# A long convolution and a soft mixture of experts on one core: x buffers no longer cleared, tables and clearings later, and the loads of a pair of steps in two bursts

## The chip, the cores and the metric

The kernel runs on one core of a Trainium2 chip. The metric is the device time of one execution in microseconds (us); lower is better. Before the change, three runs took 909.87, 915.80 and 915.04 us; their median is 915.04 us.

## The reference

A causal convolution along the sequence with a filter as long as the sequence, and then a soft mixture of experts with 8 experts of 4 slots each, all in float32:

```python
# x (8, 5696, 128), h (5696, 128)
Xf = np.fft.rfft(x, n=2 * S, axis=1); Hf = np.fft.rfft(h, n=2 * S, axis=0)
y = np.fft.irfft(Xf * Hf[None], n=2 * S, axis=1)[:, :S, :].reshape(B * S, D)
logits = y @ phi                                   # (45568, 32)
d = softmax of logits over the tokens              # columns
slot_input = d.T @ y                               # (32, 128), then per expert
slot_out[e] = np.maximum(slot_input[e] @ w1[e], 0) @ w2[e]
out = (softmax of logits over the slots) @ slot_out
```

## The kernel before, in words

The transform of length 5760 is done as 90 x 64 (`N1` x `N2`): stage A transforms over the 89 rows (`R1`) that hold data, stage B over the 64 columns, multiplies with the filter's spectrum and transforms back over the 64, and stage C transforms back over the 90 and goes on to the logits. There are nine groups: group 0 is the filter `h`, groups 1 to 8 are the eight sequences.

**Steps.** The main loop (L631) runs over steps `t`. In step `t` stage A takes one chunk of four columns, eight steps (`NJ`) to a group, 72 in all. Stage B runs nine steps behind (`LAG_B`): a group has twelve units (`NW`), one in an odd step and two in an even step. Stage C runs 27 steps behind and takes one pair of steps for one block of output, and four pairs make a sequence. The last blocks and the experts come after the loop. So an odd and an even step are one pair, with three units of stage B, two chunks of stage A and one block of stage C.

**Where data lies between stages.** `load_x` brings the input of a pair into one of two buffers `xc`, and GpSimd folds each chunk into one of three buffers `x` (`fold`, L217: the sum and the difference of a near and a far half). `stage_a` multiplies (L241), ScalarE copies the results out of PSUM (L243), and `pending` collects their stores to the array `f` in HBM, which `flush` issues: two of 60 rows in each step ("f60") and four more of 30 rows in odd steps ("f30"). `load_g` loads one unit of `f` into one of three buffers `gt` (L270). `stage_b1` multiplies it (L284) and VectorE applies the filter; `stage_b2` multiplies back (L327), and its result is stored to `zm` or, for the last units of a group, in four small stores to `zr`. `load_main` and `load_rest` bring these into `zc` and `zx` for stage C (L412, L417).

**What sets the order.** The code is issued in the order that is written, and each engine runs its own instructions in that order. Nearly every DMA is issued from SyncE's queue (SP), in the order of the code, and one that has to wait holds up all that are behind it. In the built program the DMAs use eight semaphores in turn, so that a DMA also waits for the landing of the one that used its semaphore before. `prefetch` (L638) issues a `gt` load three units ahead: unit u+3 goes into the buffer of unit u, and so stands behind `stage_b1(u)`. A group's `gt` loads may begin at the last step of the group before in stage B, for only then is all of the group's `f` on its way.

**SP's order in a pair, before.** Even step: `load_rest` of some pairs, the load of `xc`, f60 x2, `gt`, `zm` x2, the store of stage C's weights (L562), `gt`, `zm` x2. Odd step: f60 x2, `zc`, `zx`, `gt`, `zm` x2, f30 x4.

**The beginning.** Both `xc` buffers are cleared on VectorE (L176), since `h` fills only 89 of 128 rows. SP then loads `h` and the tables `wt` (L618, for `stage_b1`) and `vt` (L619, for `stage_b2`). ScalarE's queue loads `s1` and small tables, and copies a cleared tile into the rows of `zr` that are never written (L625, eight DMAs).

Of the kernel before, what the change touches and what calls it, by code (L numbers as in the profile page):

```python
# [70 lines left out]
def kernel(  # L71
# [24 lines left out]
    nc = tc.nc  # L96
    P = 128
# [5 lines left out]
    N1, N2 = 90, 64  # L103
    R1, HALF, NP = S // N2, N2 // 2, N1 // 2
    CH = 4
    NJ = HALF // CH
# [54 lines left out]
    wt = fconst.tile([P, NP, HP], F32, name="wt")  # L161
    vt = fconst.tile([P, NU, 2, HP], F32, name="vt")
# [9 lines left out]
    xs = {}  # L172
    xf = [apool.tile([P, 2, CH, D], F32, name=f"x{i}", tag=f"x{i}", bufs=1) for i in range(3)]
    xcs = [apool.tile([P, 2, 2 * CH, D], F32, name=f"xc{i}", tag=f"xc{i}", bufs=1) for i in range(2)]
    for t_ in xcs:
        nc.vector.memset(t_[:, :, :, :], 0.0)  # L176

    def load_x(m, halves=((0, 2 * CH),)):

        if 2 * m >= (B + 1) * NJ:  # L180
            return
        g, j = divmod(2 * m, NJ)
        if g == 0:
            src, blocks = h, ((0, R1 // 16 * 16), (R1 // 16 * 16, R1))
        else:
            r0 = min((g - 1) * R1, B * R1 - XR) * N2
            src, blocks = x.rearrange("b t d -> (b t) d")[r0:r0 + XR * N2], ((0, XR),)
        src = src.rearrange("(a n) d -> a n d", n=N2)
        t_ = xcs[m % len(xcs)]
        for n0, n in halves:  # L190
            a = (CH * j + n0, N2 - CH * j - n0 - n)
            p = (n0, 2 * CH - n0 - n)
            for r0, r1 in blocks:
                if n == 2 * CH:
                    v = src[r0:r1, a[0]:a[0] + n, :]
                    v = bass.AP(tensor=v.tensor, offset=v.offset,
                                ap=[v.ap[0], [(a[1] - a[0]) * D, 2], [1, n * D]])
                    nc.sync.dma_start(
                        out=t_[r0:r1, :, :, :].rearrange("p s n d -> p s (n d)"), in_=v)
                    continue  # L200
                for s_ in range(2):
                    nc.sync.dma_start(
                        out=t_[r0:r1, s_, p[s_]:p[s_] + n, :].rearrange("p n d -> p (n d)"),
                        in_=src[r0:r1, a[s_]:a[s_] + n, :].rearrange("r n d -> r (n d)"))
        xs[2 * m] = xs[2 * m + 1] = t_

# [2 lines left out]
    def fold(c):  # L209
        if c not in xs:  # L210
            return
        t_ = xs.pop(c)
        y_ = xf[c % len(xf)]
        i = CH * (c % 2)
        near, far = t_[:, 0, i:i + CH, :], t_[:, 1, ::-1, :][:, i:i + CH, :]
        for o in range(2):
            nc.gpsimd.tensor_tensor(out=y_[:, o, :, :], in0=near, in1=far,  # L217
                                    op=AL.subtract if o else AL.add)
        folded[c] = y_

# [2 lines left out]
    def flush():  # L223
        while pending:
            pending.pop(0)()
# [375 lines left out]
    NA, NC = (B + 1) * NJ, B * NJ  # L601
# [10 lines left out]
    AHEAD = 3  # L612
# [2 lines left out]
    load_x(0, ((0, CH), (CH, CH)))  # L615
    nc.scalar.dma_start(out=s1[:, :, :, :], in_=t_s1)
    load_x(1)
    nc.sync.dma_start(out=wt[:, :, :], in_=t_w)  # L618
    nc.sync.dma_start(out=vt[:, :, :, :], in_=t_v)  # L619
    nc.scalar.dma_start(out=phi[:, :], in_=moe_phi)  # L620
    nc.scalar.dma_start(out=turn[:, :, :, :, :], in_=t_turn)
    nc.scalar.dma_start(out=im[:, :, :], in_=t_im)
    nc.scalar.dma_start(out=ir[:, :], in_=t_ir)
    for i in range(8):
        nc.scalar.dma_start(  # L625
            out=zr[i // 4][i // 2 % 2, i % 2, N1 - MAIN:].rearrange("k (j r) d -> (k j) (r d)", r=2 * CH),
            in_=zring[0][1][0:4 * (HALF - N1 + MAIN), :, :, :].rearrange("p h n d -> p (h n d)"))
    fold(0)
    wait_b2 = []

    for t in range(last_front + 1):  # L631
        us = list(units(t))

        def pair(lag):
            T, half = divmod(t - LAG_C - lag, 2)
            return T if half == 0 and 0 <= T < NT else None

        def prefetch(last):  # L638
            nonlocal loaded
            while loaded < len(queue) and queue[loaded][0] <= last \  # L640
                    and queue[loaded][0] // NW * NJ + NJ <= t:
                load_g(queue[loaded][0])
                loaded += 1

        def slot_b(due=True):
            fresh = due and bool(us)
            if fresh:
                u = us.pop(0)
                stage_b1(u)
                prefetch(u + AHEAD)  # L650
                wait_b2.append(u)
            if len(wait_b2) > fresh:
                stage_b2(wait_b2.pop(0))

        T, U, V, W, X = [pair(k) for k in (0, 2, 1, 3, 5)]
        if t < NA:
            stage_a(t, False)
            fold(t + 1)
        if t == last_front:
            assert T is None and U is None  # L660
            assert pair(-1) % NQ
            flush()
            dispatch(W)
            for i in range(3):
                slot_b()
                flush()
                if i == 1:
                    softmax_sum(W)
                    stage_c2(V)
            assert not us and not wait_b2  # L670
            stage_c6(X)
            stage_c3(V)
            column_max(V)
            break
        if t % 2:
            if T is not None:
                stage_c1(T)()
            flush()
            if pair(-2) is not None:
                load_main(pair(-2))  # L680
                if pair(-2) % NQ:
                    load_rest(pair(-2))
            slot_b()
            if U is not None:
                stage_c4(U)
            if t < NA:
                stage_a(t, True)
            if U is not None:
                stage_c5(U)
                softmax_exp(U)  # L690
            flush()
        else:
            if pair(-1) is not None and pair(-1) % NQ == 0:
                load_rest(pair(-1))
            if t < NA:
                load_x(t // 2 + 2)
            flush()
            if t == NJ:
                prefetch(AHEAD - 1)
            slot_b()  # L700
            if W is not None:
                softmax_sum(W)
                dispatch(W)
            flush()
            if V is not None:
                stage_c2(V)
            if X is not None:
                stage_c6(X)
            slot_b()
            if V is not None:  # L710
                stage_c3(V)
# [221 lines left out]
```

## Time and profile before

The profiled execution took 909.23 us by the clock that gives the times above; its span in the trace is 907.4 us.

| what | value |
|---|---|
| TensorE matmuls (PE) | 760.2 us, 84% of the span |
| VectorE (DVE) | 601.4 us, 66% |
| ScalarE (ACT) | 436.8 us, 48% |
| GpSimd (POOL) | 399.8 us, 44% |
| DMA | 278.33 MB, mean 307 GB/s |
| HBM | read 147.94 MB, written 129.00 MB |

| DMA, all on SP | count | KB each |
|---|---|---|
| `gt<-f` | 99 | 512 |
| `f<-fst`, 60 rows | 144 | 240 |
| `f<-fst`, 30 rows | 144 | 120 |
| `zm<-zst` | 128 | 256 |
| `zc<-zm` | 30 | 1024 |
| `zx<-zr` | 30 | 512 |
| `xc<-in_x_dram` | 32 | 768 |
| `zr<-zst` | 96 | 128 |
| `wt<-tab_w`, `vt<-tab_v` | 1 each | 1440, 1472 |

The eight clearings `zr<-zx`, of 96 KB each, are issued from ScalarE's queue.

A group of instructions is named by engine, output and line: "PE bt L284" is the matmul of `stage_b1`. An engine's name with a q is its queue: "SPq L270" is the issue of a `gt` load. "x<-y" after DMA is a transfer from y to x. In a list of waits, the three numbers are the time waited in all, the number of waits and the longest one. In a table by windows, PE, PEld, DVE, ACT and POOL have their busy time and the number of instructions, followed by the granted clock of TensorE, the busy share of the DMA engines (packets that overlap count twice, so it can pass 1) and the rate in GB/s.

### The profile page before, as it was taken

Reading aid. Unit: us, or ns where it says so; the run is one execution under the profiler, and the core shown is the slowest. Engines: PE = TensorE matmul, PEld = TensorE weight load, DVE = VectorE, ACT = ScalarE, POOL = GpSimd, SP = SyncE. Lnnn points to the kernel's source line nnn. Section 1 sums busy time; section 2 is a strip of 40 time slices with the busy share of each in tenths; the row PEclk is TensorE's granted clock in tenths of the full one; section 3 lists DMA queues with packets and bytes.
Section 4 is the critical chain, followed back from the end, with each engine's and each line's share of the span. In section 5 each row is a group of like instructions: output and inputs, shape, how many; then the busy total and the mean of one; then the engine's idle time right before and its main releaser. Section 6 shows DMA issues by size and latency. Waiting matters only on the chain.

```text
span 907.4 us, 21291 instructions
## 1 busy us (share of the span) xinstructions
PE 760.2 (84%) x8308; PEld 387.7 (43%) x8308; DVE 601.4 (66%) x896; ACT 436.8 (48%) x880; POOL 399.8 (44%) x353
## 2 busy tenths in 40 slices
PE   6857778689999989999998999799888877767893
PEld 2212233234444444444444444344444434344793
DVE  2029767568778867886877787678778766653552
ACT  2423234335556545665655655456544444563441
POOL 4634322444555655655655566456332224651000
PEclk9979889999999999999999999899988888766855
DMA  8989999999999999999999999999998768540798
GB/s 267 318 275 343 293 296 337 298 314 376 341 291 375 361 326 308 372 358 299 357 364 335 295 373 348 303 308 346 306 291 304 264 200 341 186 166 1 292 406 335
DMA packets 170443, 278.33 MB, mean 307 GB/s; under 512 B 13543, under 2 KB 128231, under 8 KB 165135
## 3 DMA queue, kind: packets, MB, share of 16 engines
q1 hardware_dynamic: 169336, 275.74, 89.7%
q10 hardware_dynamic: 1008, 1.25, 0.5%
q8 instruction: 66, 1.08, 0.5%
q14 instruction: 33, 0.27, 0.1%
HBM read 147.94 MB, written 129.00 MB: 305 GB/s over the span
## 4 chain that ended last, share of the span: by engine, by line
PE 47%; DMA 23%; ACT 8%; POOL 8%; DVE 6%; issue 6%; SPq 1%; ACTq 0%; DVEq 0%; POOLq 0%
PE bank L241 9%; DMA gt<-f 9%; PE bt L284 9%; PE bz L327 6%; POOL y L430 5%; PE bank L412 4%; DMA f<-fst 4%; PE op L886 3%; PE bank L439 3%; PE bank L417 3%; PE bank L448 2%; DMA zx<-zr 2%; ACT fst L243 2%; DMA out_dram<-o 2%; PE bank L527 2%
## 5 line engine op out<-in xcount | busy, mean ns | idle before, releaser
L241 PE MATMUL bank<-x,s 128*32 128x512 f32 (+1 forms) x1152 | 218.0, 620 | 12.9 <-POOL x L217 8.4
L217 POOL TENSOR_TENSOR x<-xc 128x512 f32<-128x512 f32 x144 | 180.4, 1278 | 107.2 <-PE bank L241 86.5
L284 PE MATMUL bt<-gt,wt 64*64 64x256 f32 x1620 | 125.0, 419 | 72.8 <-DMA gt<-f 33.0
L430 POOL TENSOR_TENSOR y<-y,op 128x512 f32<-128x512 f32 x64 | 77.6, 1213 | 206.8 <-DVE op L404 204.3
L304 DVE TENSOR_TENSOR pi<-bt,Hi 128x1024 f32<-128x1024 f32 x96 | 113.0, 1177 | 83.5 <-PE bt L284 83.3
L243 ACT ACTIVATE fst<-bank 128x512 f32<-128x512 f32 x216 | 122.8, 592 | 86.0 <-PE bank L241 57.7
L332 ACT ACTIVATE zst<-bz 128x1024 f32<-128x1024 f32 x96 | 93.3, 972 | 128.3 <-PE bz L327 109.4
L284 PEld LDWEIGHTS bt<-gt,wt 64*64 64x64 f32 x1620 | 58.3, 141 | 151.2 <-issue 79.1
L312 DVE TENSOR_TENSOR yf<-bt,pi 128x512 f32<-128x512 f32 x192 | 119.4, 663 | 3.3
L304 DVE TENSOR_TENSOR bt<-bt,Hr 128x1024 f32<-128x1024 f32 x96 | 113.0, 1177 | 0.0
L241 PEld LDWEIGHTS bank<-x,s 128*32 128x32 f32 (+1 forms) x1152 | 55.1, 126 | 129.8 <-issue 93.6
L327 PE MATMUL bz<-yf,vt 64*64 64x256 f32 x1440 | 110.4, 404 | 0.0
L327 PEld LDWEIGHTS bz<-yf,vt 64*64 64x64 f32 x1440 | 64.3, 143 | 25.5 <-issue 4.2
L512 POOL TENSOR_TENSOR L<-L,rs 128x512 f32<-128x512 f32 x32 | 33.5, 1048 | 91.6 <-DVE rs L511 66.4
L404 DVE TENSOR_TENSOR y<-bank,y 128x512 f32<-128x512 f32 x32 | 22.1, 692 | 76.7 <-ACT y L420 76.5
L439 PE MATMUL bank<-ident,y 109*128 109x109 f32 x512 | 62.7, 273 | 7.9 <-ACT yt L441 7.9
L504 ACT ACTIVATE L<-L 128x512 f32<-128x512 f32 x32 | 20.2, 630 | 94.7 <-POOL L L501 94.6
L430 POOL TENSOR_TENSOR y<-y,om 128x512 f32<-128x512 f32 x54 | 63.9, 1183 | 2.1
L439 PEld LDWEIGHTS bank<-ident,y 109*128 109x128 f32 x512 | 52.9, 149 | 19.4 <-POOL x L217 14.7
L412 PE MATMUL bank<-zc,im 64*64 64x512 f32 x480 | 60.8, 623 | 0.0
L441 ACT ACTIVATE yt<-bank 128x360 f32<-128x360 f32 x128 | 53.0, 482 | 7.7 <-PE bank L439 7.3
L420 ACT ACTIVATE y<-bank 128x512 f32<-128x512 f32 x32 | 19.1, 596 | 72.6 <-PE bank L417 72.6
(101 smaller groups left out, 862.5 us busy)
## 6 DMA issues: line engine op xcount, KB each, us to landing
gt<-f SPq DMA_DIRECT2D x99, 512.0 KB
f<-fst SPq DMA_DIRECT2D x144, 240.0 KB
zm<-zst SPq DMA_DIRECT2D x128, 256.0 KB
zc<-zm SPq DMA_DIRECT2D x30, 1024.0 KB
xc<-in_x_dram SPq DMA_DIRECT2D x32, 768.0 KB
f<-fst SPq DMA_DIRECT2D x144, 120.0 KB
out_dram<-o SPq DMA_DIRECT2D x16, 1024.0 KB
zx<-zr SPq DMA_DIRECT2D x30, 512.0 KB
```

The source lines that it names most:

```text
L217: nc.gpsimd.tensor_tensor(out=y_[:, o, :, :], in0=near, in1=far, op=AL.subtract if o else AL.add)
L241: nc.tensor.matmul(p[i * m:(i + 1) * m, :], s1[:, g // B, q + o, cols], columns(c_, o), start=True, stop=True)
L243: nc.scalar.activation(st[:, :, q, :], p[:, :].rearrange("p (n d) -> p n d", d=D), AF.Copy)
L284: nc.tensor.matmul(bt[q * HP:(q + 1) * HP, a, o, :], wt[r, 2 * i + q, :], t_[r, 2 * o + q, :, :].rearrange("p c d -> p (c d)"), start=True ...
L304: nc.vector.tensor_tensor(out=p_, in0=pv, in1=h_, op=AL.mult)
L312: nc.vector.tensor_tensor(out=y_[r, 0:k, c, :], in0=pv[:, :, c, :], in1=pi[r, 0:k, 1 - c, :], op=op_)
L327: nc.tensor.matmul(bz[a * HP:(a + 1) * HP, q, o, :], vt[r, i, a, :], y_[r, a * m + o, :, :].rearrange("p c d -> p (c d)"), start=True, sto ...
L332: nc.scalar.activation(st[:, 0:m, 0:n, :].rearrange("p o q x -> p q o x"), bz[:, 0:n, 0:m, :], AF.Copy)
L412: nc.tensor.matmul(ps[o, c][h_ * HP:(h_ + 1) * HP, :], im[r, c, :], zt[r, h_, :, c, :], start=True, stop=False)
L430: eng.tensor_tensor(out=part_, in0=part(v, 0), in1=o_[:, :, :], op=sign)
L439: nc.tensor.transpose(p[:, i * TR:(i + 1) * TR], ys[T][0:TR, k * CH + i, 0:D], ident[0:TR, 0:TR])
L441: nc.scalar.activation(yt[:, k * CH:(k + 1) * CH, :, :], of_tokens(p), AF.Copy)
```

## The change

1. The two `xc` buffers are not cleared. Instead rows 96 to 127 of the three `x` buffers are, the fold works on 96 rows, and each load of `h` gets a third block: its last seven rows once more, put into rows 89 to 95 (a table has zeros there).
2. `wt` is loaded in step 3 and `vt` in step 9. The clearings of `zr` move from ScalarE's queue to SP, two in each of the steps 11, 13, 15 and 17.
3. In an even step the loads come in one burst behind the first `stage_b1`: the pending stores (f60 x2), `load_rest`, `xc`, and one `gt`. The even step's second `gt` load is no longer issued behind the second `stage_b1`, but in the next odd step, ahead of that step's own `gt`. SP's order in a pair becomes, in the even step, f60 x2, `zx` of some pairs, `xc`, `gt`, `zm` x2, the store of L562, `zm` x2; and in the odd step f60 x2, `zc`, `zx`, `gt` x2, `zm` x2, f30 x4. The order on TensorE, VectorE, ScalarE and GpSimd stays as it is but for what points 1 and 2 name.

```diff
-    for t_ in xcs:
-        nc.vector.memset(t_[:, :, :, :], 0.0)
+    for t_ in xf:
+        nc.vector.memset(t_[XR:P, :, :, :], 0.0)
...
         if g == 0:
-            src, blocks = h, ((0, R1 // 16 * 16), (R1 // 16 * 16, R1))
+            last = R1 // 16 * 16
+            src, blocks = h, ((0, last, 0), (last, R1, last), (2 * R1 - XR, R1, R1))
...
-            for r0, r1 in blocks:
+            for r0, r1, p0 in blocks:
+                p1 = p0 + r1 - r0
...
-        near, far = t_[:, 0, i:i + CH, :], t_[:, 1, ::-1, :][:, i:i + CH, :]
+        near, far = t_[0:XR, 0, i:i + CH, :], t_[0:XR, 1, ::-1, :][:, i:i + CH, :]
...
-    nc.sync.dma_start(out=wt[:, :, :], in_=t_w)
-    nc.sync.dma_start(out=vt[:, :, :, :], in_=t_v)
...
-    for i in range(8):
-        nc.scalar.dma_start(
+    def clear_rest(i):
+        nc.sync.dma_start(
...
-        def slot_b(due=True):
+        def refill():
+            if wait_b2:
+                prefetch(wait_b2[-1] + AHEAD)
+
+        def slot_b(loads=refill, due=True):
             fresh = due and bool(us)
             if fresh:
                 u = us.pop(0)
                 stage_b1(u)
-                prefetch(u + AHEAD)
                 wait_b2.append(u)
+                loads()
...
             flush()
+            if t == 3:
+                nc.sync.dma_start(out=wt[:, :, :], in_=t_w)
+            if t == NJ + 1:
+                nc.sync.dma_start(out=vt[:, :, :, :], in_=t_v)
+            if NJ + 2 < t < NJ + 11:
+                clear_rest(t - NJ - 3)
+                clear_rest(t - NJ - 2)
             if pair(-2) is not None:
                 load_main(pair(-2))
                 if pair(-2) % NQ:
                     load_rest(pair(-2))
+            refill()
             slot_b()
...
         else:
-            if pair(-1) is not None and pair(-1) % NQ == 0:
-                load_rest(pair(-1))
-            if t < NA:
-                load_x(t // 2 + 2)
-            flush()
-            if t == NJ:
-                prefetch(AHEAD - 1)
-            slot_b()
+            def burst():
+                flush()
+                if pair(-1) is not None and pair(-1) % NQ == 0:
+                    load_rest(pair(-1))
+                if t < NA:
+                    load_x(t // 2 + 2)
+                if t == NJ:
+                    prefetch(AHEAD - 1)
+                refill()
+
+            if not us:
+                burst()
+            slot_b(burst)
...
-            slot_b()
+            slot_b(lambda: None)
```

More of the change, by code (lines that the diff above doesn't have):

```diff
@@ L183, in load_x @@
         if g == 0:
-            src, blocks = h, ((0, R1 // 16 * 16), (R1 // 16 * 16, R1))
+            last = R1 // 16 * 16
+            src, blocks = h, ((0, last, 0), (last, R1, last), (2 * R1 - XR, R1, R1))
         else:
             r0 = min((g - 1) * R1, B * R1 - XR) * N2
-            src, blocks = x.rearrange("b t d -> (b t) d")[r0:r0 + XR * N2], ((0, XR),)
+            src, blocks = x.rearrange("b t d -> (b t) d")[r0:r0 + XR * N2], ((0, XR, 0),)
         src = src.rearrange("(a n) d -> a n d", n=N2)
@@ L198, in load_x @@
                     nc.sync.dma_start(
-                        out=t_[r0:r1, :, :, :].rearrange("p s n d -> p s (n d)"), in_=v)
+                        out=t_[p0:p1, :, :, :].rearrange("p s n d -> p s (n d)"), in_=v)
                     continue
@@ L202, in load_x @@
                     nc.sync.dma_start(
-                        out=t_[r0:r1, s_, p[s_]:p[s_] + n, :].rearrange("p n d -> p (n d)"),
+                        out=t_[p0:p1, s_, p[s_]:p[s_] + n, :].rearrange("p n d -> p (n d)"),
                         in_=src[r0:r1, a[s_]:a[s_] + n, :].rearrange("r n d -> r (n d)"))
@@ L214, in fold @@
         i = CH * (c % 2)
-        near, far = t_[:, 0, i:i + CH, :], t_[:, 1, ::-1, :][:, i:i + CH, :]
+        near, far = t_[0:XR, 0, i:i + CH, :], t_[0:XR, 1, ::-1, :][:, i:i + CH, :]
         for o in range(2):
-            nc.gpsimd.tensor_tensor(out=y_[:, o, :, :], in0=near, in1=far,
+            nc.gpsimd.tensor_tensor(out=y_[0:XR, o, :, :], in0=near, in1=far,
                                     op=AL.subtract if o else AL.add)
```

## The prediction

> **What bounds the kernel now.** First the page's slices of the span, to see which resource is full where.
>
> ```profile
> PE   6857778689999989999998999799888877767893
> DMA  8989999999999999999999999999998768540798
> ```
>
> Each digit is 22.7 us. The DMA engines are at 9 from the third slice to the thirtieth, and PE is at 9 in most of slices 9 to 29. So the beginning (to 180 us) is a matter of transfers, and from 206 to 650 us, where all three stages run, two resources are full at once. The change touches nothing behind 740 us, where the last `gt` has been used.
>
> Second, the chain of waits for the first 60 us: start, length, what.
>
> ```profile
> 6.83 3.22 DMA zr<-zx
> 10.07 8.41 DMA wt<-tab_w
> 18.91 9.80 DMA f<-fst
> ...
> 49.24 7.52 DMA gt<-f
> 56.80 1.98 PE bt L284 x16
> ```
>
> One transfer hands over to the next until stage B begins at 56.80. The timeline of the first 20 us shows the queues:
>
> ```profile
> 0.73 0.35 ACTq L616 DMA_DIRECT2D s<-tab_s  x1
> 3.02 3.71 SPq L202 DMA_DIRECT2D xc<-in_h_dram  x8
> 6.24 6.53 ACTq L625 DMA_DIRECT2D zr<-zx  x8
> 12.80 1.28 ACT L243 ACT_TABLE_LOAD   x1 [12.80 <-DMA zr<-zx]
> ```
>
> ScalarE's queue issues its first DMA at 0.73 us, SP only at 3.02, behind the clearing; eight loads take it 3.71 us, 0.46 each.
>
> Third, TensorE's waits, over the whole span and then from 206 to 650 us alone (two answers):
>
> ```profile
> PE bt L284 <- DMA gt<-f: 33.0, 10, 10.2
> ```
>
> ```profile
> PE bt L284 <- DMA gt<-f: 13.1, 5, 5.5
> ```
>
> Of the 33.0 us that `stage_b1` waits for `gt`, 10.2 are the one wait before 56.80. In the loop there are five waits, of 0.5, 3.4, 2.1, 1.7 and 5.5 us by windows around each, all at a group's first unit. Between them PE is busy 19.24 us in most windows of 20. So the loop's excess over TensorE's own pace is 13.1 us.
>
> Fourth, windows; the last three numbers are the granted clock, the DMA share and GB/s.
>
> ```profile
> 28.00:58.00 30.00, 19.67 (x92) 6.51 (x96) 0.00 (x0) 10.36 (x19) 15.74 (x13) 0.84 0.98 325
> 58.00:64.00 6.00, 6.00 (x36) 1.28 (x32) 3.65 (x4) 1.89 (x4) 1.87 (x2) 0.71 0.61 191
> 58.00:103.00 45.00, 35.71 (x300) 11.80 (x292) 41.28 (x48) 14.33 (x24) 19.83 (x16) 0.96 0.95 306
> 206.00:650.00 444.00, 416.97 (x4764) 199.54 (x4760) 339.35 (x516) 254.90 (x517) 247.36 (x211) 0.98 1.00 337
> 524.60:529.00 4.40, 4.22 (x76) 3.09 (x76) 3.74 (x6) 2.53 (x5) 4.28 (x4) 1.00 1.05 413
> 534.00:540.00 6.00, 6.00 (x73) 2.38 (x70) 3.39 (x8) 2.48 (x5) 0.39 (x1) 1.00 1.01 341
> ```
>
> The engines are as busy at 341 as at 413 GB/s. 524.6 to 529 is where SP has just issued `zc`, `zx` and `gt`, loads in a row; 534 to 540 is `xc`, f60 x2 and `gt`, loads and stores mixed.
>
> **The beginning, part by part.** The sum starts from the profiled 909.23 us; the median is 5.81 us above it, and I carry the difference over.
>
> The clearing: SP could issue from 0.73 instead of 3.02, a gain of 2.3 us at most. But the first pair's load is twelve DMAs instead of eight: 0.73 + 12 x 0.46 = 6.3 against 3.02 + 3.71 = 6.7, 0.4 at least. For its first half, six against four, it is 3.5 against 4.9. I take this 1.4. The new clearings, 3 x 32 rows x 1024, have their nearest row in the clearing of `zx` (128x1024, 0.91 us): 2.7 us against 3.5 removed, on a VectorE that then idles 51.29 us until stage B, so nothing. The fold on 96 rows lies between 1278 x 96/128 = 959 ns and the 1278 ns of its row; I take 1278, since the columns are unchanged, and beyond the very first fold no wait of a PE matmul is put down to it. The last-seven-rows loads add 4 x 14 + 3 x 56 = 224 KB, 0.7 us at the 325 GB/s of 28 to 58 us.
>
> `vt` (1472 KB) and the clearings (8 x 96 KB) leave the queue ahead of stage B: 2.29 MB, 7.1 us at 325 GB/s. That counts because the chain up to 56.80 is transfers alone. `wt` is merely shifted within it: nothing, as its 8.41 us from issue to landing are covered by the six steps to its first use; without them PE would wait those 8.4. ScalarE's queue loses 6.53 us of issuing, and its first copy out of PSUM no longer starts at 12.80; this makes stores ready earlier, but they join the same full DMA, so nothing more. Stage B begins 1.4 + 7.1 - 0.7 = 7.8 us earlier, at 49.0.
>
> Then it comes back. `vt` and six of the eight clearings stand on SP ahead of the first `gt` of group 1: 2.10 MB, 6.5 us. From 58 to 103 us DVE is busy 41.28 of 45 and DMA 0.95, so little hides them, but from 58 to 64 us the share is only 0.61, as SP waits there for step 10; `vt` stands just before, and fills 0.39 x 6 = 2.3 us. The last two clearings (0.6 us) fall behind 105 us, where 5% of 103 us is free: nothing. SP's issuing of eight more DMAs, 8 x 0.46 = 3.7 us, delays the `gt` behind each pair of them by 0.9; its cover is that SP waits for the DMA engines there anyway, and without it up to 3.7 would be lost. Sum of the beginning: -7.8 + 6.5 - 2.3 = -3.6 us, with bounds of 0 (all comes back, and the gain of SP's start with it) and -7.8 (all hidden).
>
> The Trainium skill ("DMA: Bandwidth & Descriptors", section "Issuing engines are not separate DMA queues") says that DMAs of different issuers run on the same 16 engines and that the issuer only changes sequencer time. That speaks against a gain from moving the clearings off ScalarE, and the sum has none from that; by the rule alone only their delay counts.
>
> **The loop.** SP's issues of `gt` in one pair, and the PE row that uses the middle one's data (two views):
>
> ```profile
> 535.66 0.39 SPq L270 DMA_DIRECT2D gt<-f  x1
> 538.80 0.72 SPq L270 DMA_DIRECT2D gt<-f  x1
> 544.86 0.38 SPq L270 DMA_DIRECT2D gt<-f  x1
> ```
>
> ```profile
> 550.51 1.09 PE L284 MATMUL bt<-gt,wt 64*64 64x256 f32 x16
> ```
>
> Loads in a row: a pair turns from loads to stores four times now and twice afterwards. If the mixed 6.0 us of `xc` and f60 ran at 413 instead of 341 GB/s, they would take 5.0: 1.0 us a pair, 22 over 22 pairs, more than all the 13.1 us of waits, which are the most that can be had, as PE is full between them. Half of the turns go, so I take half, 6.5. Bounds: 0 (the order makes no rate) and 13.1. With these waits gone, what is late next is PE itself.
>
> The Trainium skill (the same page, section "Where 436 GB/s comes from") has an HBM side of about 358 GB/s that binds transfers between HBM and SBUF; by it no order beats the present pace, and the loop's term would be 0. The windows here reach 413, and the measurement decides.
>
> What is moved: the middle `gt` goes from 538.80 to just ahead of 544.86, past two `zm` stores, f60 x2, `zc` and `zx`, which move up. Its cover shrinks from 550.51 - 538.80 = 11.7 to about 6.1 us. What a landing takes no row says directly: at least 1.3 us (512 KB at 413 GB/s), at most the 7.1 to 8.1 between issue and use where PE waited. So a stall of 0 to 2.0 us in a pair. I take 0 in the sum, since a stalled PE lets the queue catch up, and the next load then lands earlier. f60 ahead of `xc` makes `xc` wait for ScalarE's copies: SP's waits for them are 42.1 us in 45, 0.9 each; `gt` was behind f60 already, and the fold needs `xc` two steps later, so nothing, or 0.9 a pair if GpSimd had no slack (it idles over half the time). From 650 to 740 us the DMA share is down to 0.87, so the moved loads have room there: nothing.
>
> Sum: 909.2 - 3.6 - 6.5 = 899.1 profiled; with 5.8, a median of **905 us**.
>
> **Rivals.** *Only the beginning counts*: loads and stores mix in the DMA engines whatever order they are issued in, so the bursts don't do what they say, and the five waits stay. For it: the share is 1.0 already, and SP issues stores while loads issued several us earlier are still on their way. Against: the 72 GB/s between the two stretches. 915.0 - 3.6 = 911.4, from 907 to 915. *The moved load comes too late*: from the point where a landing takes over 6.1 us, `stage_b1` in the second slot of every even step waits for `gt`, a wait that no row has now. For it: 7.1 us at the boundaries. Against: those stand behind `xc`, the queue's worst stretch. At the middle, 1.0 us a pair, 22 - 3.6 gives 933; at 0.5 it is 922.
>
> **The numbers.** Forecast 0.45, only the beginning 0.37, too late 0.18. The forecast's own bounds are 915.0 - 20.9 = 894 to 911; the range goes on to 922, over the first rival and the small end of the second. This kernel's runs differ by 0.65%, so about 1% (905.9 to 924) is what can be told from no change; part of the forecast lies above 905.9, and part of the first rival just below. Faster 0.45, same 0.39, slower 0.16.
>
> **What would show it.** First L284 at 49 us and that of group 1 at 101 instead of 105; the loop's L284 waits for `gt` at half of 13.1 us, still at the groups' first units, and a rate from 206 to 650 us above 337 GB/s. New L284 waits in mid-group would prove the last rival, five unchanged ones the first. It would be wrong altogether if the step's SP waits for ScalarE left the DMA engines idle, to be seen as a share under 1.0.

## The result, and the profile after

The changed kernel takes 947.9 us (median of four runs, 947.03 to 949.81) beside 915.42 us for the kernel before (four runs): a ratio of 1.036, interval 1.030 to 1.042. It is slower by 32.5 us, where 905 us had been forecast, and lies beyond the 922 us at which the forecast's range ended. The profiled execution took 948.67 us, its span is 946.9 us.

First the chain of waits of the changed kernel for the first 60 us (start, length, what).

```profile
1.20 4.34 DMA xc<-in_h_dram
5.56 1.66 DMA xc<-in_h_dram
...
8.66 7.79 PE bank L243 x32
...
25.69 8.93 DMA f<-fst
...
49.04 7.54 DMA gt<-f
...
56.63 1.99 PE bt L286 x16
```

Stage B begins at 56.63 us, as before (56.80). Matmuls of stage A and the folds on GpSimd now stand in the chain from 7 to 26 us, where before it held transfers alone from 6.83 us on.

Then the windows of the changed kernel, with the columns of those before.

```profile
28.00:58.00 30.00, 17.08 (x81) 4.74 (x80) 0.00 (x0) 7.55 (x14) 12.35 (x10) 0.86 0.98 326
58.00:103.00 45.00, 35.70 (x292) 11.99 (x284) 37.63 (x42) 13.14 (x22) 19.81 (x16) 0.91 0.99 319
206.00:650.00 444.00, 399.85 (x4404) 190.82 (x4396) 315.20 (x477) 235.46 (x474) 234.26 (x200) 0.95 0.99 317
```

From 206 to 650 us the DMA engines are still at 0.99, but they move 317 GB/s and not 337, and PE is busy 17 us less. Same share and less moved: a packet takes longer. In the traces' packet records of 18 pairs of steps, those of 1 KB (`gt` and `zm`) take 52.9 ns in the mean, and 47.2 before. TensorE's waits in this stretch:

```profile
PE bt L286 <- DMA gt<-f: 15.8, 10, 3.9
PE bank L419 <- DMA zx<-zr: 14.5, 5, 4.5
```

The waits for `gt` are now ten and not five, and there are new ones for `zx`. Of the 15.8 us, 5.9 stand in mid-group, in six waits, and the others at groups' first units. Two pairs of the chain from 380 us on show how long a middle `gt` takes:

```profile
385.72 8.17 DMA gt<-f
393.89 0.14 issue
394.02 1.09 PE bt L286 x16
...
398.67 6.95 DMA zm<-zst
405.62 0.02 issue
405.63 9.32 DMA gt<-f
414.96 0.14 issue
415.09 1.09 PE bt L286 x16
```

The moved load takes 8.17 and 9.32 us to land, and TensorE starts on it 0.13 us later. That is the length of the transfer and not what TensorE lost: from 393 to 395 and from 414 to 416 us it waited only 0.2 and 0.8 us (two answers).

```profile
PE bt L286 <- DMA gt<-f: 0.2, 1, 0.2
```

```profile
PE bt L286 <- DMA gt<-f: 0.8, 1, 0.8
```

The issue at 405.63 itself comes behind the landing of a `zm` store (6.95 us).

Where the 39.5 us between the two spans arise, by the starts of step 27 and step 71 of stage A: 12.6 us ahead of step 27 (184.0 became 196.6), 28.7 us in steps 27 to 71 (455.3 became 484.0), and -1.8 behind them. (Two expectations below have 195.7 and 481 where this count gives 196.6 and 484.0.)

### The profile page after: what moved, and what is told of

It reads as the page before. It is cut to its first block, busy times and chain, and to the rows that moved or that the text cites. A ratio compares the mean times of both kernels' runs of the same rounds, so it can differ in the third digit from the quotient of the medians.

```text
span 946.9 us, 21261 instructions
## 1 busy us (share of the span) xinstructions
PE 778.4 (82%) x8308; PEld 392.0 (41%) x8308; DVE 601.0 (63%) x897; ACT 438.3 (46%) x880; POOL 399.4 (42%) x353
## 4 chain that ended last, share of the span: by engine, by line
PE 42%; DMA 36%; ACT 5%; issue 5%; POOL 4%; DVE 4%; SPq 2%; DVEq 0%; ACTq 0%; POOLq 0%
DMA gt<-f 16%; PE bank L243 11%; PE bt L286 9%; DMA zm<-zst 6%; PE bz L329 6%; DMA zx<-zr 5%; DMA out_dram<-o 4%; PE bank L414 3%; PE bank L441 3%; DMA f<-fst 2%; PE bank L419 2%; POOL y L432 2%; PE bank L450 2%; PE bank L529 2%; ACT zst L334 1%
## 5 line engine op out<-in xcount | busy, mean ns | idle before, releaser
L243 PE MATMUL bank<-x,s 128*32 128x512 f32 (+1 forms) x1152 | 224.8, 636 | 13.3 <-POOL x L219 13.3
L219 POOL TENSOR_TENSOR x<-xc 96x512 f32<-96x512 f32 x144 | 180.0, 1274 | 118.5 <-PE bank L243 96.9
L286 PE MATMUL bt<-gt,wt 64*64 64x256 f32 x1620 | 131.2, 436 | 82.0 <-DMA gt<-f 42.7
L286 PEld LDWEIGHTS bt<-gt,wt 64*64 64x64 f32 x1620 | 60.9, 147 | 164.0 <-issue 92.6
L329 PE MATMUL bz<-yf,vt 64*64 64x256 f32 x1440 | 113.2, 410 | 0.0
L329 PEld LDWEIGHTS bz<-yf,vt 64*64 64x64 f32 x1440 | 66.6, 146 | 26.3 <-issue 6.3
```

What stands on the lines that cost most here:

```text
L219: nc.gpsimd.tensor_tensor(out=y_[0:XR, o, :, :], in0=near, in1=far, op=AL.subtract if o else AL.add)
L243: nc.tensor.matmul(p[i * m:(i + 1) * m, :], s1[:, g // B, q + o, cols], columns(c_, o), start=True, stop=True)
L286: nc.tensor.matmul(bt[q * HP:(q + 1) * HP, a, o, :], wt[r, 2 * i + q, :], t_[r, 2 * o + q, :, :].rearrange("p c d -> p (c d)"), start=True ...
L329: nc.tensor.matmul(bz[a * HP:(a + 1) * HP, q, o, :], vt[r, i, a, :], y_[r, a * m + o, :, :].rearrange("p c d -> p (c d)"), start=True, sto ...
```

## The experiments

**Which part.** Four kernels have a part of the change each: points 1 and 2, point 3, and the two halves of point 3, which are the move of `gt` and f60 ahead of `xc`. Before took 912.75 us beside them.

Points 1 and 2 alone (the clearings, the tables; the loop as before):

> Points 1 and 2 of the change (no clearing of xc, tables and clearings later), with the loop's order as before. If the beginning loses by itself what the two traces differ by at step 27 (195.7 against 184.0 us): 927 us, and the loop's TensorE waits for gt as before (13 us from 206 to 650). If that difference is the loop's order showing already in stage B's first groups: 911 to 915 us, with group 1's first L286 at 101 to 105 us.

Measured: 914.35 us, ratio 1.0018 (0.9981 to 1.0055). The first L284 starts at 54.8 instead of 56.8, and that of group 1 at 105.3, where it was before (105.2). So 2.0 us are won and given back within one group. In five other traces with the beginning as before, the two starts stand at 57.5 to 59.4 and at 106.2 to 107.3 us; so the gain may be up to 4.5 us, of which up to 2.0 may stay. Two windows tell why it is not 7.8, here of this kernel, and below of the kernel before:

```profile
0.00:10.00 10.00, 1.47 (x3) 0.54 (x5) 4.79 (x9) 1.28 (x1) 3.52 (x10) 1.00 0.58 137
10.00:20.00 10.00, 9.85 (x43) 3.70 (x42) 0.00 (x0) 4.78 (x8) 7.43 (x7) 1.00 0.92 259
```

```profile
0.00:10.00 10.00, 1.64 (x3) 0.58 (x5) 5.58 (x8) 0.00 (x0) 3.69 (x10) 1.00 0.68 175
10.00:20.00 10.00, 10.00 (x43) 4.16 (x41) 0.00 (x0) 5.74 (x9) 6.99 (x6) 1.00 1.02 373
```

Without `wt`, `vt` and the clearings the DMA engines have less to do for 20 us (137 and 259 GB/s against 175 and 373), as stage A is still folding and multiplying (PE is busy 9.85 of 10 us from 10 us on) and SP issues the first store of `f` only at 13.75 us. The transfers that left had filled time that others use little. `wt` itself is still in the chain, with 8.43 us from 24.07 us on.

Point 3 alone (the whole order of the loop, the beginning as before):

> Point 3 alone (the bursts), with the beginning as before. If the loop's order is the cause of all: 945 to 948 us. If it is the cause of the 28.7 us between steps 27 and 71 alone: 940 to 944 us, with a DMA rate near 317 GB/s in the loop.

Measured: 947.16 us, 1.0354 (1.0286 to 1.0422). It is all of the loss. Its two halves:

```diff
 # gt_only: the even step's second gt, in the next odd step
+            refill()
             slot_b()                  # odd step
...
-            slot_b()                  # even step, second
+            slot_b(lambda: None)
```

> The middle gt load alone is moved into the odd step; xc stays ahead of the two f60 stores. The late load as the cause (a landing takes 8 to 9 us, its cover is about 6): 935 to 945 us, with TensorE waits for gt in mid-group. The lower DMA rate behind f60-before-xc as the cause: 915 to 920 us.

```diff
 # f60_first: even step
+            flush()
             if t < NA:
                 load_x(t // 2 + 2)
-            flush()
```

> The two f60 stores alone go ahead of the load of xc; every gt load stays where it was. The lower DMA rate as the cause (stores first, then xc and gt loads without stores between them, which run at 170 to 300 GB/s in the trace of the change): 935 to 945 us and about 320 GB/s in the loop. The late load as the cause: 913 to 918 us and 337 GB/s.

Measured: the moved `gt` alone 935.25 us, 1.0226 (1.0164 to 1.0288); the stores ahead of `xc` alone 941.0 us, 1.0298 (1.0236 to 1.036). Both lose, and they don't add up: 2.3% and 3.0% make 3.5%. The windows and waits from 206 to 650 us tell them apart, the moved `gt` first:

```profile
206.00:650.00 444.00, 402.62 (x4516) 192.93 (x4516) 319.58 (x487) 238.59 (x483) 235.92 (x201) 0.97 0.98 323
```

```profile
PE bt L284 <- DMA gt<-f: 23.6, 11, 3.9
```

```profile
28.00:58.00 30.00, 20.22 (x80) 6.53 (x80) 0.00 (x0) 10.66 (x19) 17.35 (x14) 0.85 0.89 277
206.00:650.00 444.00, 408.02 (x4574) 194.58 (x4568) 326.16 (x492) 243.81 (x489) 243.47 (x208) 0.96 1.00 326
```

```profile
PE bt L284 <- DMA gt<-f: 16.3, 4, 4.8
```

With the moved `gt` there are 11 waits, seven of them in mid-group with 19.2 of the 23.6 us, and the DMA share falls to 0.98. The reading is that the engines wait for the load, and the DMA engines for the engines; the DMAs alone, below, agree with it. With the stores ahead of `xc` the waits for `gt` barely grow (16.3 against 13.1) and the share is 1.00, yet 326 GB/s are moved: the packets themselves are slower. In the trace's packet records of steps 27 to 71 those of 1 KB (`gt` and `zm`) take 52 ns and not 47. And it loses 11.1 us before step 27 already (184.0 became 195.1): at 28 to 58 us the share is 0.89. SP issues the loads of `h` for the third and fourth pair behind stores, at 17.30 and 29.55 us instead of 13.11 and 26.71, and up to 206 us GpSimd waits 19.9 us for loads of `h`, where it had waited 10.0.

**Cover for the moved load.** A fourth `gt` buffer lets each load be issued a unit, some 6 us, earlier.

```diff
-        t_ = bpool.tile([P, 4, 2, D], F32, name="gt", tag="gt", bufs=3)
+        t_ = bpool.tile([P, 4, 2, D], F32, name="gt", tag="gt", bufs=4)
...
-    AHEAD = 3
+    AHEAD = 4
```

> The kernel before with a fourth `gt` buffer and `prefetch` four units ahead instead of three (the 4 KB come from letting stage C's small store tile share the tile `d`). It is the reference for the three runs beside it. Theory 'late loads' (where this loop loses time, TensorE waits for a `gt` that was issued too late): the waits for `gt` in 206 to 650 us are 13.1 us already without it and stand at the groups' first units, where a fourth buffer does not let the load start earlier; so 905 to 915. Theory 'rate' (the loop loses where the DMA engines move less): DMA share 1.0 and 337 GB/s stay, so 910 to 918.

> The moved middle `gt` alone, with the fourth buffer: every `gt` is issued one unit (about 6 us) earlier, so the moved load has again about the cover that it had before the move. Theory 'late loads': the 2.3% of this move come back, 912 to 920, and the waits for `gt` from 206 to 680 us fall from 23.6 to under 14 us. Theory 'rate' (two `gt` in a row are served worse): cover does not help, 930 to 938, waits for `gt` or for the loads behind them stay above 20 us.

> The two f60 stores ahead of `xc`, the `gt` loads as before, with the fourth buffer. Theory 'rate' (the order itself makes the packets of 1 KB slower, 52 instead of 47 ns, at a full DMA share): 934 to 942, steps 27 to 71 still 470 us or more. Theory 'late loads' (the loss is `gt` landing behind `xc`): 912 to 922, steps 27 to 71 near 456 us and 1 KB packets back at 47 ns.

> The changed kernel with the fourth buffer. Theory 'late loads' alone: all comes back, 912 to 922. Theory 'rate' alone: 944 to 950 as without it. Both, one for each half of the change (late loads for the moved `gt`, rate for the stores ahead of `xc`): it falls to what the stores ahead of `xc` cost alone, 934 to 942.

Measured: 926.52, 933.31, 944.83 and 947.85 us, beside 913.26 for before. The first missed all expectations: 1.0145 (1.0108 to 1.0181), although the waits for `gt` from 206 to 650 us are down to 0.5 us. So the other three can be read only beside it: the moved `gt` costs 6.8 us there, the stores ahead of `xc` 18.3 and the change 21.3. The largest wait of the first is new:

```profile
PE bank L439 <- DVE acc L532: 18.0, 9, 2.0
```

I put it down to the place found for the 4 KB (stage C's store tile shares the tile `d`), and repeated the pair with another place, the part of the filter's spectrum that no unit uses.

> The kernel before with a fourth `gt` buffer and `prefetch` four units ahead; the 4 KB come from putting the tile `d` into the part of the filter's spectrum that no unit uses, which adds no wait. Theory 'the DMAs bound the loop': the 13.1 us of waits for `gt` go, but the DMA engines are full, and the DMAs alone need 98.6% of the loop's time, so 905 to 913. Theory 'waits bound it': 898 to 903.

> The same with the middle `gt` moved. Theory 'late loads': with the cover restored what is left is what the DMAs alone lose by this order, 3.5 us in 18 pairs, some 5 in all: 0.3 to 0.8% over the run with the fourth buffer beside it, instead of 2.3%. Theory 'rate': 1.8% or more over it.

Measured: 920.95 us, 1.0092 (1.0057 to 1.0127), and 926.72 us, 1.0163 (1.0106 to 1.0221). The waits of the first from 206 to 650 us:

```profile
PE bank L439 <- DVE acc L535: 10.0, 5, 2.0
PE bank L417 <- DMA zx<-zr: 9.0, 4, 3.1
PE bt L284 <- DMA gt<-f: 5.8, 4, 1.8
```

So the shared tile was only part of it: 10.0 us of the wait for `acc` stay. 7.3 us of waits for `gt` go, and 19 us of others come; the kernel with four buffers is slower than with three, and both theories for it missed. The moved `gt` costs 5.8 us here (926.72 - 920.95, 0.6%, as 'late loads' had it), and 22.5 us without the cover (935.25 - 912.75). So about three quarters of its cost go with more cover; that none of it is merely hidden under the waits that the fourth buffer brings is not shown. With the stores ahead of `xc` the first set gives 18.3 us (944.83 - 926.52) for 28.3 without the fourth buffer: most of that stays.

**The DMAs alone.** In four kernels the engines' work of steps 27 to 71 is left out, and the DMAs go on in their order.

```diff
+        nc = muted if 3 * NJ + 3 <= t < NA else loud
...
+        if nc is not loud:
+            loud.vector.memset(v, 0.0)     # each tile that is stored
```

> The kernel before with the work of TensorE, VectorE, ScalarE and GpSimd left out in steps 27 to 71: there all DMAs run in their order and with their addresses, and of the engines only a clearing of each tile that is stored is left, on VectorE. It gives what the DMA engines alone make of this order. With the engines the steps 27 to 71 took 455.3 us at 338 GB/s. Theory 'the DMAs bound this stretch' (share 1.0): still 440 to 455 us. Theory 'TensorE bounds it': clearly less, down to 373 us at the 413 GB/s of the clumps of loads.

> The same work left out, in the kernel with the middle `gt` moved alone (476.7 us in these steps with the engines). Theory 'late loads' (TensorE waits for a load with too little cover): without TensorE no difference to the DMAs of the order before, within 1%. Theory 'rate' (the order itself is served worse): 3% or more longer.

> The same work left out, in the kernel with the f60 stores ahead of `xc` alone (474.9 us with the engines). Theory 'rate': 3 to 5% longer than the DMAs of the order before, with packets of 1 KB at 50 ns or more against 47. Theory 'coupling' (the packets are slow because stores and loads wait for the engines and then fall together): within 1% of the order before.

> The same work left out, in the changed kernel (481 us with the engines). Theory 'rate': as long as the DMAs of the f60 order, 3 to 6% over the order before. Theory 'coupling': within 1% of the order before.

The windows reach from SP's issue of the 13th `xc` load of `x` to that of the 31st, 18 pairs: the order before, the moved `gt`, f60 ahead of `xc`, and the changed order.

```profile
206.60:569.20 362.60, 0.00 (x0) 0.00 (x0) 171.57 (x250) 0.00 (x0) 0.00 (x0) 0.50 1.01 346
```

```profile
209.10:575.20 366.10, 0.00 (x0) 0.00 (x0) 171.57 (x250) 0.00 (x0) 0.00 (x0) 0.50 1.01 342
```

```profile
214.00:589.10 375.10, 0.00 (x0) 0.00 (x0) 171.57 (x250) 0.00 (x0) 0.00 (x0) 0.50 1.01 333
```

```profile
215.90:598.40 382.50, 0.00 (x0) 0.00 (x0) 171.57 (x250) 0.00 (x0) 0.00 (x0) 0.50 1.01 326
```

One execution each. PE did nothing at all in these windows, and the same bytes take nearly as long as with it. The clearings that are left make SP wait some 31 us from 206 to 570 us in the order before and 27 with f60 ahead, at a share of 1.01 in both, so they don't make the difference. The same 18 pairs of the full kernels before and after the change:

```profile
205.40:573.30 367.90, 348.81 (x4002) 167.44 (x4003) 285.35 (x435) 213.48 (x432) 210.28 (x179) 0.99 1.01 342
217.70:612.70 395.00, 359.21 (x3972) 170.92 (x3965) 282.16 (x427) 211.96 (x427) 207.88 (x177) 0.95 0.99 317
```

All four orders:

| order | DMAs alone, us | against before | with the engines, us | against before |
|---|---|---|---|---|
| before | 362.6 | | 367.9 | |
| middle `gt` moved | 366.1 | +3.5 | 388.5 | +20.6 |
| f60 ahead of `xc` | 375.1 | +12.5 | 385.7 | +17.8 |
| the change | 382.5 | +19.9 | 395.0 | +27.1 |

The DMAs need 98.6% of the time of the loop before; all that TensorE could give back by waiting less is 5.3 us. That is beside one execution, a quick one: in the kernel with points 1 and 2 alone, whose loop has the order before, the 18 pairs took 374.2 us, which makes it 96.9% and 11.6 us. The stores ahead of `xc` lose 12.5 of their 17.8 us in the DMAs alone, the moved `gt` 3.5 of 20.6, and the change 19.9 of 27.1. So 'rate' holds for the stores (3.4% longer) and the change (5.5%), and 'late loads' for the moved `gt` (1.0%). In the packet records, 44,164 packets of 1 KB take 52.0 ns each with f60 ahead and 46.9 before: 5.1 ns x 44,164 / 16 engines = 14.1 us, which covers the 12.5.

**Addresses or company.** In two kernels of the same kind the order changes from group to group. The expectations count a group from SP's issue of its first f60 store to that of the next group's; but where neighbouring groups differ in order, such a stretch holds three to five loads of `xc`. The windows here go from the last f30 store of the group before to the group's own last, which stands at the same place in every order and leaves four loads of `xc` in each. In the order before, group 3 took 78.7 to 79.2 us in four such kernels, so a difference below 1 us tells nothing. Groups 4 to 7 in the order before:

```profile
243.43:325.23 81.80, 0.00 (x0) 0.00 (x0) 38.21 (x56) 0.00 (x0) 0.00 (x0) 0.50 1.01 341
325.23:405.97 80.74, 0.00 (x0) 0.00 (x0) 38.21 (x56) 0.00 (x0) 0.00 (x0) 0.50 1.01 344
405.97:486.61 80.64, 0.00 (x0) 0.00 (x0) 38.21 (x56) 0.00 (x0) 0.00 (x0) 0.50 1.01 346
486.61:568.88 82.27, 0.00 (x0) 0.00 (x0) 38.21 (x56) 0.00 (x0) 0.00 (x0) 0.50 1.00 340
```

With f60 ahead of `xc` they take 83.6, 84.9, 85.1 and 84.1 us.

```diff
 # addresses: xc from one stretch of x; f written to one stretch for each store
+  in_=bass.AP(tensor=v.tensor, offset=src.offset, ap=[[2 * n * D, r1 - r0], [n * D, 2], [1, n * D]])
+  out=bass.AP(tensor=fd[g].tensor,
+              offset=fd[g].offset + (16 * LOW * high + (k1 - k0) * (2 * (c_ % NJ) + o)) * 2 * CH * D,
+              ap=[[2 * CH * D, k1 - k0], [1, 2 * CH * D]])
 # places: load_x behind the first gt; at the end of the even step; behind the odd step's gt; between the two f60
```

> The DMAs alone (engine work left out in steps 27 to 71), a different variant in each group, from the first f60 store of a group to that of the next; in the order before these groups took 81.8, 80.7, 80.6 and 82.3 us (groups 4 to 7), in the f60 order 83.7, 84.8, 85.1 and 84.2. Group 4: order before, with `xc` read from one stretch of `x` instead of rows 32 KB apart (other data, same sizes and packets). Group 5: f60 ahead of `xc`, `xc` read from one stretch. Group 6: order before, `f` written to one stretch for each store instead of rows 64 KB apart. Group 7: f60 ahead of `xc`, addresses as they are. Theory 'addresses of xc': group 4 falls to 79 or less, and group 5 is no longer than it, at most 81. Theory 'addresses of f': group 6 falls to 78 or less. Theory 'order alone': group 4 stays at 81 to 82, group 5 at 84 to 85, group 6 at 80 to 81.

Groups 4 to 7:

```profile
243.65:323.49 79.84, 0.00 (x0) 0.00 (x0) 38.21 (x56) 0.00 (x0) 0.00 (x0) 0.50 1.02 347
323.49:407.34 83.85, 0.00 (x0) 0.00 (x0) 38.21 (x56) 0.00 (x0) 0.00 (x0) 0.50 1.01 334
407.34:488.95 81.61, 0.00 (x0) 0.00 (x0) 38.21 (x56) 0.00 (x0) 0.00 (x0) 0.50 1.01 341
488.95:572.75 83.80, 0.00 (x0) 0.00 (x0) 38.21 (x56) 0.00 (x0) 0.00 (x0) 0.50 1.01 335
```

Reading `xc` from one stretch saves 2.0 us of 81.8 in the order before, and 1.1 of 84.9 with f60 ahead, where 3.1 us of loss over the order before (80.74) stay. So the place of `xc`'s rows doesn't make the loss by order. Whether the place has a price of its own is not shown, for against the expectation the packets changed too: the group has some 600 packets of 4 KB fewer and 290 of 8 KB more, as the two halves of a row now lie side by side. The places of `f` have no price (81.6 against 80.6).

> The DMAs alone, `xc` in another place in each group; in the order before (`xc`, f60 x2, `gt`) 81.8, 80.7, 80.6 and 82.3 us for groups 4 to 7. Group 4: f60 x2, `gt`, `xc`, `zm`. Group 5: at the end of the even step, behind the second `gt` and ahead of its `zm`. Group 6: in the odd step, behind `zc`, `zx` and `gt`. Group 7: f60, `xc`, f60, `gt`. Theory 'a load must not follow a load of another pitch' (loads in a row get in each other's way): groups 4 and 6 slow, 84 or more, group 7 as before or quicker. Theory 'stores in a row are what is slow' (f30 x4 and f60 x2 without a load between): groups 4, 5 and 6 all at 84 or more, group 7 between. Theory 'xc belongs into quieter company': group 5 or 6 under 80.

```profile
241.78:325.45 83.67, 0.00 (x0) 0.00 (x0) 38.21 (x56) 0.00 (x0) 0.00 (x0) 0.50 0.99 331
325.45:409.28 83.83, 0.00 (x0) 0.00 (x0) 38.21 (x56) 0.00 (x0) 0.00 (x0) 0.50 0.99 331
409.28:498.22 88.94, 0.00 (x0) 0.00 (x0) 38.21 (x56) 0.00 (x0) 0.00 (x0) 0.50 1.00 318
498.22:579.77 81.55, 0.00 (x0) 0.00 (x0) 38.21 (x56) 0.00 (x0) 0.00 (x0) 0.50 1.01 342
```

`xc` beside other loads is slower by 1.9, 3.1 and 8.3 us, most where four loads stand in a row (`zc`, `zx`, `gt`, `xc`); between the two f60 it is as before (81.55 against 82.27). A quieter place was not found. In the three slow orders the six stores of `f` also stand in a row, so one more kernel has each alone, and two orders with more turns.

```diff
+  if V_ == "f60_f60_gt_zm_xc_zm": pending.pop(0)(); load_x(t // 2 + 2)    # group 4, behind slot_b
+  "xc_gt_f60_f60": flush() behind slot_b          # group 5
+  "xc_f60_gt_f60": pending.pop(0)() ahead of slot_b   # group 6
+  "f60_zc_f60_zx_gt": pending.pop(0)(); load_main; flush(); load_rest     # group 7, odd step
```

> The DMAs alone (engine work left out in steps 27 to 71), the order within a pair changed by group; the order before (f30 x4, `xc`, f60 x2, `gt`) took 81.8, 80.7, 80.6 and 82.3 us for groups 4 to 7, and `xc` behind f60 was 1.9 to 8.3 us longer in four places where, each time, six stores of `f` stood in a row and two loads as well. Group 4: f60 x2, `gt`, `zm`, `xc`, `zm`: six stores in a row, but no two loads. Group 5: `xc`, `gt`, f60 x2: two loads in a row, but no six stores of `f` (four, and then two). Group 6: `xc`, f60, `gt`, f60: more turns than before. Group 7: in the odd step f60, `zc`, f60, `zx`, `gt` in place of f60 x2, `zc`, `zx`, `gt`. Theory 'six stores in a row': group 4 84 or more, group 5 at most 82. Theory 'two loads in a row': group 4 at most 82, group 5 84 or more. Theory 'every turn between loads and stores helps': groups 6 and 7 shorter than 80. Theory 'turns cost' (the prediction's): groups 6 and 7 longer than 82 and 84.

```profile
242.09:324.24 82.15, 0.00 (x0) 0.00 (x0) 38.21 (x56) 0.00 (x0) 0.00 (x0) 0.50 0.99 334
324.24:408.06 83.82, 0.00 (x0) 0.00 (x0) 38.21 (x56) 0.00 (x0) 0.00 (x0) 0.50 1.02 339
408.06:487.71 79.65, 0.00 (x0) 0.00 (x0) 38.21 (x56) 0.00 (x0) 0.00 (x0) 0.50 1.01 349
487.71:566.15 78.44, 0.00 (x0) 0.00 (x0) 38.21 (x56) 0.00 (x0) 0.00 (x0) 0.50 1.02 351
```

Six stores in a row alone cost 0.3 us (82.15 against 81.80), which tells nothing, and two loads in a row alone 3.1 (83.82 against 80.74), of the 4.2 that f60 ahead costs in that group. The packets of 1 KB agree: 51.2 ns in the mean with two loads in a row, 48.8 with six stores, 46.9 before, and 51.7 to 52.4 with f60 ahead. So 'two loads in a row' fits best, though both its marks (82 and 84) are missed by 0.2 us, and each order stood in one group of one execution. It is not every load, either: the moved `gt` puts two behind `zc` and `zx` and costs 3.5 us in 18 pairs, 0.8 a group. In all the orders that are slow by more, `xc` stands beside a `gt`.

More turns are no cost: with f60 on either side of `gt` it is 79.65 against 80.64 (1.0, at the edge of what tells nothing), and with f60 between `zc` and `zx` 78.44 against 82.27.

**An order with one turn more, in the whole kernel.**

```diff
 # odd step: f60, zc, f60, zx, gt in place of f60 x2, zc, zx, gt
-            flush()
+            if pair(-2) is not None and pending:
+                pending.pop(0)()
+            else:
+                flush()
             if pair(-2) is not None:
                 load_main(pair(-2))
+                flush()
```

> The kernel before with one edit in the odd step: f60, `zc`, f60, `zx`, `gt` in place of f60 x2, `zc`, `zx`, `gt`; all else as before. In the DMAs alone this took 79.1 instead of 82.3 us a group (1 KB packets 46.7 ns). Theory 'every turn between loads and stores helps, and the DMAs bound the loop': 3.2 us a group in 5.5 groups, 17.6 us, 893 to 903 against 912 or so; rate from 206 to 650 us 343 GB/s or more. Theory 'TensorE is the next bound, as it is busy 19.24 of 20 us': at most the 13.1 us of its waits for `gt`, and 1 to 6 us of them, 905 to 911. Theory 'noise of one group in one run': within 0.3% of before. Against all: `zc` stands one f60 later, whose cover is the two steps until stage C uses it; if that is short, TensorE waits for `zc` or `zx`, 915 to 925.

Measured: 907.87 us (12 runs) beside 914.37 (17 runs), ratio 0.9929, interval 0.9896 to 0.9963. It beats both kernels, by 6.5 us over the kernel before and some 40 over the changed one. That is between what the DMAs alone would give (17.6 us) and nothing, in the range of the expectation with TensorE as the next bound. That TensorE is this bound is not shown, and its profile can't say where the time went: the profiled execution took 915.1 us, the longest of the twelve, and shows 335 GB/s from 206 to 650 us and the same 13.1 us of waits for `gt` as before.

## Why the prediction was wrong

**What bounds the loop.** The prediction took the loop's excess over TensorE's own pace, 13.1 us of waits, as all that order could change, and the DMA engines, at a share of 1.0, as something that follows. With TensorE idle the same DMAs take 362.6 of 367.9 us. The DMAs set the pace, and TensorE is busy beside them for nearly as long (348.8 us). So 13.1 us was no ceiling for a loss, and waits were no measure of it. (The page's row for DMA was misread by one slice: its third digit is 8, and the nines begin with the fourth. Nothing hangs on that.)

**"Loads in a row run at 413 GB/s."** This is the step that failed most. The term was -6.5 us; the order by itself costs +19.9 in 18 pairs of the DMAs alone. 413 GB/s belong to `zc`, `zx` and `gt` at the place where they stand, not to loads as such: a fourth load, `xc`, beside them took the group from 346 to 318 GB/s. The two windows compared different packets (the first has 0.88 of its 1.82 MB in packets of 8 KB, the second none), and the difference was read as one of order. The statement that half of the turns go, and half of the waits with them, has the wrong sign: one turn more took a group of the DMAs alone from 82.3 to 78.4 us, and the whole kernel down by 0.7%.

**The moved `gt`.** What the rival "the moved load comes too late" had named came: mid-group waits, and landings of 8.17 and 9.32 us where the point of decision was 6.1. The sum had taken 0 "since a stalled PE lets the queue catch up"; with the move alone the queue did not, as it moved 323 GB/s at a share of 0.98 where it had moved 337 at 1.00. Alone the move costs 22.5 us; with cover 5.8. That this is near the rival's 22 is luck: the rival had 1.0 us in each of 22 pairs, and the trace has seven mid-group waits of 0.6 to 3.9 us, six of them at a group's sixth unit. In the change as a whole, where the transfers are slower, mid-group waits come to 5.9 us only.

**f60 ahead of `xc`.** Taken as nothing, or 0.9 us a pair, for SP's waits alone. It costs 28.3 us alone: the slower packets in the loop, and 11.1 us before step 27. There GpSimd's slack, named as the cover, wasn't enough: TensorE's waits for the fold (`POOL x`) grow from 8.4 us in one to 15.7 in five. The 11.1 us compare one trace each; the last kernel above, with the order before up to there, began step 27 at 190.4 and not 184.0 us, so 5 to 11 is what the traces bear.

**The beginning.** Forecast -3.6 us, measured +1.6 with an interval of -1.7 to +5.0 (0.9981 to 1.0055 of 912.75): about nothing. Of its steps, that it comes back was right; the first L284 was to be at 49.0 and stood at 54.8 in the kernel with the beginning alone. The term that failed is 7.1 us for 2.29 MB that leave the queue. It held "because the chain up to 56.80 is transfers alone"; with those transfers gone, the next chain is stage A's folds and matmuls and then `wt`, and it is only 2.0 us shorter (4.5 at most, by the other traces). With the changed loop it comes to 56.6, as the loop's order alone had put it at 61.1.

**The rivals.** "Only the beginning counts" named order as without effect, and fell with the rest. "Too late" had the right sign and 922 to 933 us; what it lacked was that the order also slows the packets. The chances left out the case that came: in none of the three could the order itself make the transfers longer.

**The figure that was set aside.** The prediction had weighed the Trainium skill ("DMA: Bandwidth & Descriptors", section "Where 436 GB/s comes from"), with its 358 GB/s between HBM and SBUF, and set it aside for a window of 413. That by this figure no order beats the present pace was misread: 358 is 6% over the 337 of the loop. Over whole groups no order here passed 351 GB/s (group 7 of the last kernel of DMAs alone), while a slice of 22.7 us of the page before has 376; so no run contradicts the figure for a mixture over a whole group, and shorter stretches do. That order can't do harm, it doesn't say, and below the figure order made 318 to 351.

**What stays open.** Why `xc` beside a `gt` makes the packets of 1 KB slower: that the two read from places that get in each other's way was tried only for the rows of `xc`, and those rows are not it. Each DMA also waits for the landing of the one that used its semaphore, eight before it, so order decides what is on its way at once as well; no run changed that. Why the two halves of the change don't add up with the engines (22.5 and 28.3 make 34.4 us), though in the DMAs alone they do, and more (3.5 and 12.5 make 19.9): it fits that slower transfers leave TensorE slack under which a late load hides, but no run shows it. What the granted clock of TensorE has to do with it: in the 18 pairs it is 0.99 before, 0.97 with either half and 0.95 with the change. It may be a part of what the DMAs alone leave unexplained (17.1 us for the moved `gt`, 7.2 for the change), or follow from TensorE's waits; no run separates them, and the DMAs alone, with TensorE idle, are free of it. Where the waits for `acc` and `zx` come from with a fourth buffer: all of TensorE's waits from 206 to 650 us grow by 9.3 us (26.1 to 35.4), which covers the 8.1 that the kernel loses. And where in the whole kernel the last order wins its 6.5 us.

## What to carry to other kernels

Before costing a reorder, find out which resource sets the pace by taking the other's work away: here the DMAs alone needed 97 to 98.6% of the loop's time, and any order has then to be priced as transfers. Loads and stores in one full queue did best here when they alternated, and rates of short windows say which packets stand there, not what an order is worth. A load that is moved is to be priced by the landings seen in a full queue (here 8 to 9 us against 6.1 of cover), and of transfers taken out of a start-up, the price is what the engines' own chain behind them leaves.

## What was not expected of the hardware

- At the same bytes and a DMA share of 0.99 to 1.02 the rate of a group of transfers ranged from 318 to 351 GB/s by nothing but the order in one queue. The busy share does not see it, as the packets themselves get longer (1 KB: 46.9 to 53.3 ns in the mean of 18 pairs).
- `xc` from one stretch instead of rows 32 KB apart made its group 2.0 us (2%) shorter, with larger packets as well, so that the share of either is open. The Trainium skill ("DMA: Bandwidth & Descriptors", section "Latency and other measured facts") has copies at row pitches of 2 MiB and more, powers of two, as slower than at a padded pitch; no run here has such a pitch. The rows of `f`, 64 KB apart, cost nothing that could be told (81.6 against 80.6 us).
- One more buffer for the loads that TensorE waits for took 7.3 us of those waits away and made the kernel 0.9% slower (920.95 against 912.82 us).
